# More units of a convolution channel-major, output copies on two engines, taps and jobs at other steps, before a SwiGLU block

One core of one Trainium2 chip. The metric is the time of one execution on the device in microseconds (us). Executions in the fast state are compared throughout (the record marks one as slow when it takes over 1.5% more than the fastest of the same kernel; that happened once, in e4_best); every number of a stall or a block is read from the trace of one profiled execution.

## The reference

A causal convolution of 7 taps over x (8 x 4096 x 192), the taps being a softmax over each head's weights (8 heads of 24 channels), then a SwiGLU feed-forward block with a width of 1536:

```python
w = softmax(weight)                        # 8 heads x 7 taps
out = np.einsum('hk,bskhg->bshg', w, x_unf)      # x_unf: 7 shifted copies of zero-padded x
x = out.reshape(32768, 192)
g = x @ w_gate                             # 192 x 1536
silu = g * (1.0 / (1.0 + np.exp(-g)))
return (silu * (x @ w_val)) @ w_out        # 1536 x 192
```

## The kernel before

The 32768 tokens are 64 blocks of 512; four blocks are a unit. A block is worked off in 12 steps ("chunks" of the 1536 columns, step n = 12 b + j): six gate/val matmuls on TensorE, a silu on ScalarE, a product h on VectorE. Behind chunks 1, 4, 7 and 10 stand the acc matmuls ("slots"), which multiply earlier h by w_out.

The convolution runs ahead of the blocks, in two forms. Some units are convolved on TensorE with band matrices. The others, `POOLED`, are channel-major: GpSimd casts x to fp16 in DRAM (`cast_x`), SyncE loads it transposed (`turn_x`), and six jobs per unit compute the taps with a per-channel scale: taps 0 and 3 on ScalarE, 1 and 2 on VectorE, 4 to 6 and all remaining adds on GpSimd. Four copies on SyncE's queue then put a block's result where the matmuls read it (`place`).

Names in the code and the traces: xs is the fp16 x in DRAM, x its transposed tiles, total, part and piece the sums of a job, y the result of a job for a pair of blocks; pxc is what gate and val matmuls read for a channel-major block, xc the same for a unit convolved on TensorE, which passes through DRAM (scr) and is fetched by transposes; sig is the silu, o_sb the output; the picks are small masks for the taps' scales, made once in the start-up.

```python
POOLED = (2, 3, 5, 6, 8, 9, 11, 12, 14, 15)
...
def turn_x(u, i, at):
    ...
    t = cpool.tile([P, TB + XP], fp16, tag=tag, name=tag, bufs=6)
    seq(nc.sync.dma_start_transpose(out=t, in_=rows[:, at : at + P]))
    ...
def planned(v):                      # v: a channel-major unit; s0: its first step
    s0 = ustep * v
    cast, jobs = {2: (19, 44), 3: (40, 60)}.get(v, (s0 - 118, s0 - 95))
    turns = ((0, 0), (0, Q), (2, Q), None, (1, 0), (1, Q), (3, Q), None, (2, 0), (3, 0))
    lead = {2: (33, 1), 3: (49, 1)}.get(v, (cast + 7, 2))    # first step, distance
    # cast at step `cast`, turn m at lead[0] + lead[1] * m, jobs queued at step `jobs`
...
def pooled_work(n, j, busy):         # after each step
    ...
    if not busy:
        ready = dve_steps[0][0] if dve_steps else None
        ahead = act_steps[0][0] if act_steps else n_jobs[0]
        if ready is not None and (j in (4, 10) or (j in (1, 7) and ready < ahead)):
            dve_steps.pop(0)[1]()                            # one tap on VectorE
        if j in (1, 7, 10) and act_steps and (ready is None or ahead < ready + 3):
            act_steps.pop(0)[1]()                            # one tap on ScalarE
...
# slot 4, behind chunk 4: the end of the previous block
seq(nc.scalar.copy(o_sb[:, 0:2, :], acc[b][0]))
seq(nc.scalar.copy(o_sb[:, 2:4, :], acc[b][1]))
```

In these traces the queues go in program order, and one that stands at a wait holds up what is behind it.

Of the kernel before, what the change touches and what calls it, by code (L numbers as in the profile page):

```python
# [10 lines left out]
def kernel(  # L11
# [9 lines left out]
    nc = tc.nc  # L21
    fp32 = mybir.dt.float32
    fp16 = mybir.dt.float16
    i32 = mybir.dt.int32
    AF = mybir.ActivationFunctionType
    ALU = mybir.AluOpType
# [5 lines left out]
    H, K = weight.shape  # L32
    NT = B * S
    Dff = moe_w_gate.shape[1]
    P = 128
    Q = 64
    SL = D // Q
    grp = D // H
    SUBS = 4
    TB = P * SUBS  # L40
# [9 lines left out]
    ER = ((0, 3), (3, 5))  # L50
    XW = 2 * EG * EO
    NU = NT // UT
    POOLED = (2, 3, 5, 6, 8, 9, 11, 12, 14, 15)
    upb = S // UT
    n_blocks = NT // TB
    n_steps = n_blocks * NCH
# [16 lines left out]
    def seq(i):  # L73

        e = i.ins.engine
        if e in last_on:
            tc.add_manual_dep(i.ins, last_on[e].name, NOSYNC, reason="order")
        last_on[e] = i.ins
        return i

    wpool = ctx.enter_context(tc.tile_pool(name="wts", bufs=1))
    cpool = ctx.enter_context(tc.tile_pool(name="conv", bufs=2))
# [29 lines left out]
    def xe_tile(e):  # L112
        xe[e] = cpool.tile([P, 6, D], fp16, tag="xe", name="xe", bufs=4)
# [62 lines left out]
    def load_wo(m):  # L176
        seq(
            nc.gpsimd.dma_start(
                out=wo16[:, E * m : E * m + E, :].rearrange("p e d -> p (e d)"),
                in_=moe_w_out[WF * m : WF * m + WF, :].rearrange(  # L180
                    "(p e) d -> p (e d)", p=P
                ),
            )
        )

    def small(name, shape, dt=fp32):
        return wpool.tile(shape, dt, tag=name, name=name)
# [14 lines left out]
    load_w(2)  # L202
    for m in range(3):
        load_wo(m)
    xe_tile(2)
    xe_load(2)
    xe_tile(3)
# [32 lines left out]
    def make_shift(n):  # L240
# [26 lines left out]
            op=ALU.mult,  # L267
# [8 lines left out]
            op0=ALU.mult,  # L276
# [257 lines left out]
    pick = {}  # L534

    def make_picks():
        for name, first, rows in (("c01", 0, P), ("c2", P, Q)):
            which = small(f"which_{name}", [H, P], i32)
            seq(
                nc.gpsimd.iota(  # L540
                    which,
                    pattern=[[0, P // rows], [1, rows]],
                    base=first,
                    channel_multiplier=-grp,
                )
            )
            low = small(f"low_{name}", [H, P])
            seq(nc.vector.tensor_single_scalar(low, which, 0, op=ALU.is_ge))
            pick[name] = small(f"pick_{name}", [H, P], fp16)
            seq(  # L550
                nc.vector.scalar_tensor_tensor(
                    pick[name], which, float(grp), low, op0=ALU.is_lt, op1=ALU.mult
                )
            )

# [40 lines left out]
    def turn_x(u, i, at):  # L596
        rows = xs[u][TB * i : TB * i + TB + XP]
        tiles = (x01, x12)[at // Q]
        tag = f"x{at // Q}"
        t = cpool.tile([P, TB + XP], fp16, tag=tag, name=tag, bufs=6)  # L600
        seq(nc.sync.dma_start_transpose(out=t, in_=rows[:, at : at + P]))
        tiles[u, i] = t

# [111 lines left out]

    def planned(v):
        s0 = ustep * v
        cast, jobs = {2: (19, 44), 3: (40, 60)}.get(v, (s0 - 118, s0 - 95))
        turns = (
            (0, 0), (0, Q), (2, Q), None, (1, 0), (1, Q), (3, Q), None, (2, 0), (3, 0)  # L720
        )
        lead = {2: (33, 1), 3: (49, 1)}.get(v, (cast + 7, 2))
        plan.setdefault(cast, []).append(lambda: cast_x(v))
        for m, turn in enumerate(turns):
            if turn:
                todo = lambda turn=turn: turn_x(v, *turn)
            else:
                todo = lambda i=m // 4: join_x(v, i)
            plan.setdefault(lead[0] + lead[1] * m, []).append(todo)
        plan.setdefault(jobs, []).append(lambda: queue_jobs(v))  # L730

    def pooled_work(n, j, busy):
        step_now[0] = n
        if not busy:
            ready = dve_steps[0][0] if dve_steps else None
            ahead = act_steps[0][0] if act_steps else n_jobs[0]
            if ready is not None and (
                j in (4, 10) or (j in (1, 7) and ready < ahead)
            ):
                dve_steps.pop(0)[1]()  # L740
            if j in (1, 7, 10) and act_steps and (ready is None or ahead < ready + 3):
                act_steps.pop(0)[1]()
        while placing:
            u, i = placing[0]
            need = (u, "block", i), (u, "pair", i % 2)
            if not all(job in finished for job in need):
                break
            done = max(finished[job] for job in need)
            if n < max(done + 14, ustep * u + NCH * i - 16):
                break  # L750
            placing.pop(0)
            place(u, i)
# [72 lines left out]
    def slot(k, b, after=None, between=None):  # L825

        if k == 1:
            acc[b] = [
                apool.tile([P, 2, D], fp32, tag=f"acc{i}", name=f"acc{i}")
                for i in range(2)  # L830
            ]
            down(b, [(False, G[0])], 1, after)
            if between is not None:
                between()
            down(b, [(False, G[1])], 1, None)
        elif k == 2:
            down(b, [(True, G[0]), (True, G[1])], 0, after)
            if between is not None:
                between()
            if b < n_blocks - 1:  # L840
                down(b, [(False, G[2])], 0, None)
        elif k == 3:
            down(b, [(True, G[2])], 1, after)
            if between is not None:
                between()
            down(b, [(False, G[3])], 1, None)
        else:
            down(b, [(True, G[3])], 0, after)
            o_sb = hpool.tile([P, SUBS, D], fp32, tag="o_sb", name="o_sb", bufs=3)
            seq(nc.scalar.copy(o_sb[:, 0:2, :], acc[b][0]))  # L850
            seq(nc.scalar.copy(o_sb[:, 2:4, :], acc[b][1]))  # L851
            t0 = b * TB
            seq(
                nc.sync.dma_start(
                    out=out[t0 : t0 + TB, :].rearrange("(s p) d -> p s d", p=P),
                    in_=o_sb,
                )
            )
            del acc[b]
# [26 lines left out]
    for n in range(n_steps):  # L886
        b, j = divmod(n, NCH)
        u, ls = divmod(n, ustep)
        work = None
        if n in (12, 19):  # L890

            def work(e=2 if n == 12 else 3):
                early(e, (gate_bank, gate_bank, val_bank))

        at = (25, 31) if u == 0 else (10, 22)
        if u + 1 < NU and not pooled(u + 1) and ls in at:

            def work(u=u, hh=at.index(ls)):
                conv_half(u + 1, hh)

        gate_val(n)
        if n == 6:
            early(1, (*acc_banks, gate_bank))
        elif n == 8:
            eturn(1, (*acc_banks, gate_bank))
        elif n in (9, 12, 15, 17):
            k = {9: 1, 12: 2, 15: 3, 17: 4}[n]
            slot(k, 0, silu[n - 1 if k == 4 else n - 2], work)
        elif j % 3 == 1 and n > 18:
            k = {1: 3, 4: 4, 7: 1, 10: 2}[j]  # L910
            slot(k, b - 1 if j < 7 else b, silu[n - 2], work)
        if n == 18:
            eturn(2, (*acc_banks, gate_bank))
        elif n == 20:
            eout(3)
        elif n == 21:
            efetch(3)
        if n == 24:
            make_picks()
        if n == 33:  # L920
            make_channel_taps()
        for job in plan.pop(n, ()):
            job()
        pooled_work(n, j, work is not None)
        if u + 1 < NU and not pooled(u + 1):
            if ls == at[0]:
                conv_dup(u + 1)
            if ls == at[1]:
                for m in range(2):
                    conv_out(u + 1, m)  # L930
            if ls == at[1] + 1:
                for m in range(2, 8):
                    conv_out(u + 1, m)
            lo = 32 if u == 0 else 28
            if ls in range(lo, lo + 12, 3):
                fetch(UB * (u + 1) + (ls - lo) // 3)
        if u + 2 < NU and not pooled(u + 2):
            if ls == (21 if u == 0 else 1):
                x16_tile(u + 2)
                load_x(u + 2, 0, silu[n - 1])  # L940
            if ls == (23 if u == 0 else 5):
                load_x(u + 2, 1, silu[n - 1])
            if ls == (37 if u == 0 else 26):
                dup_x(u + 2)
# [42 lines left out]
```

## Time and profile before

| | before |
|---|---|
| time, median of 3 (range) | 792.96 us (792.71 to 793.93) |
| span of the profiled execution | 791.8 us |
| 64 blocks of 11.73 us | 750.7 us |
| stalls behind chunk 7 | 11.7 us, in 24 blocks |

From the page of the kernel before: busy time of each engine, the granted clock in 40 slices (9 is 90% or more), and four groups of instructions (count, then busy time and mean ns of one, then idle time of the engine ahead of them):

```profile
span 791.8 us, 27799 instructions
...
PE 775.6 (98%) x11371; PEld 521.7 (66%) x11371; DVE 638.4 (81%) x949; ACT 588.6 (74%) x1054; POOL 500.7 (63%) x485
...
PEclk9999999999999999999999999999999999999999
...
L792 PE MATMUL acc<-wo,h 64*128 64x192 f16 x6096 | 300.4, 243 | 9.8 <-DVE h L777 7.9
...
L651 DVE SCALAR_TENSOR_TENSOR total<-x,both_taps,total 128x512 f32<-128x512 f16 x120 | 130.4, 1087 | 0.0
...
L676 ACT ACTIVATE total<-x,both_taps 128x512 f32<-128x512 f16 x60 | 42.8, 714 | 2.6 <-DMA x<-xs 2.6
...
L851 ACT COPY o_sb<-acc 128x384 f32<-128x384 f32 x63 | 30.6, 486 | 0.0
```

TensorE is busy for 98% at full clock; no other engine is near its limit on average. What can be had is in the stalls and in TensorE's own share of the convolution. 120 taps stand on VectorE at a mean of 1.09 us, and ScalarE waits once for a transposed x (2.6 us).

### The profile page before, as it was taken

The page shows a single profiled execution, that of the slowest core. Times are in us where ns is not written, and L with a number is a line of the kernel's source. Part 1 is how long each engine was busy: PE and PEld are TensorE (multiplying, and loading weights), DVE is VectorE, ACT ScalarE, POOL GpSimd, SP SyncE. Part 2 cuts the span into 40 slices and gives each one's busy share as a digit, 9 for nine tenths or more (in the row PEclk, how much of TensorE's full clock was granted, in tenths as well). Part 3 has the DMA queues.
Part 4 walks back from the last instruction along what each step waited for, and adds up shares of the span by engine and source line. Part 5 has one row for each costly group of instructions (what it writes and reads, how often), then busy time and mean ns, then how long its engine had stood idle before and what let it go on. Part 6 is the DMA issues. An engine that isn't in the chain of part 4 may idle for free.

```text
span 791.8 us, 27799 instructions
## 1 busy us (share of the span) xinstructions
PE 775.6 (98%) x11371; PEld 521.7 (66%) x11371; DVE 638.4 (81%) x949; ACT 588.6 (74%) x1054; POOL 500.7 (63%) x485
## 2 busy tenths in 40 slices
PE   8999999999999999999999999999999999999997
PEld 5666666666666666666666666666666666666665
DVE  6677889888888867888896688898767888886665
ACT  6677787877878767777876678788668787876664
POOL 8102999996899920589995047899802689990000
PEclk9999999999999999999999999999999999999999
DMA  9965538355642394386129638631862653221211
GB/s 140 177 141 99 124 106 166 83 123 129 115 109 69 56 201 109 94 130 133 39 68 174 117 83 155 107 92 46 146 144 78 150 123 76 68 64 40 68 55 41
DMA packets 159840, 83.90 MB, mean 106 GB/s; under 512 B 102552, under 2 KB 159136, under 8 KB 159136
## 3 DMA queue, kind: packets, MB, share of 16 engines
q1 hardware_dynamic: 139216, 65.58, 35.4%
q0 software_dynamic: 20496, 16.54, 15.0%
q8 instruction: 89, 1.46, 0.8%
q14 instruction: 39, 0.32, 0.1%
HBM read 33.08 MB, written 38.60 MB: 91 GB/s over the span
## 4 chain that ended last, share of the span: by engine, by line
PE 94%; DVE 2%; issue 1%; SPq 1%; DMA 0%; ACT 0%; DVEq 0%; ACTq 0%
PE gate L766 60%; PE acc L792 30%; DVE h L777 2%; PE val L766 2%; PE cv L462 1%; PE warm L867 1%; DMA x<-xs 0%; SPq L520 0%; PE turn L431 0%; PE cv L373 0%; SPq L498 0%; PE acc L813 0%; ACT tme L391 0%; ACT wide L331 0%; ACT sig L775 0%
## 5 line engine op out<-in xcount | busy, mean ns | idle before, releaser
L777 DVE TENSOR_TENSOR h<-sig,val 128x512 f16<-128x512 f16 x768 | 500.0, 685 | 143.5 <-PE val L766 123.1
L775 ACT ACTIVATE sig<-gate 128x512 f16<-128x512 f32 x768 | 455.3, 599 | 183.0 <-PE val L766 155.9
L766 PEld LDWEIGHTS <-w 64*128 64x128 f16 x4608 | 255.6, 110 | 182.3 <-issue 1.5
L766 PE MATMUL val<-pxc,w 64*128 64x512 f16 x1440 | 337.2, 376 | 0.0
L766 PE MATMUL gate<-pxc,w 64*128 64x512 f16 x1440 | 337.2, 376 | 0.0
L792 PE MATMUL acc<-wo,h 64*128 64x192 f16 x6096 | 300.4, 243 | 9.8 <-DVE h L777 7.9
L792 PEld LDWEIGHTS <-h 64*128 64x128 f16 x6096 | 257.7, 94 | 73.9 <-DVE h L777 13.3
L766 PE MATMUL val<-xc,w 64*128 64x512 f16 x864 | 203.6, 376 | 0.3 <-DVE h L777 0.3
L766 PE MATMUL gate<-xc,w 64*128 64x512 f16 x864 | 203.6, 376 | 0.0
L626 POOL TENSOR_TENSOR total<-total,piece 128x512 f32<-128x512 f32 x120 | 158.4, 1320 | 10.0
L641 POOL TENSOR_SCALAR piece<-x,both_taps 128x512 f32<-128x512 f16 x180 | 146.1, 812 | 0.0
L651 DVE SCALAR_TENSOR_TENSOR total<-x,both_taps,total 128x512 f32<-128x512 f16 x120 | 130.4, 1087 | 0.0
L626 POOL TENSOR_TENSOR total<-total,part 128x512 f32<-128x512 f32 x60 | 81.0, 1349 | 69.6 <-DVE total L651 53.9
L490 POOL COPY tm<-tm 128x1280 f16<-128x1280 f16 x5 | 6.2, 1249 | 125.5 <-DVE tm L479 125.5
L626 POOL TENSOR_TENSOR pxc<-total,piece 128x512 f16<-128x512 f32 x40 | 55.8, 1396 | 3.3
L676 ACT ACTIVATE total<-x,both_taps 128x512 f32<-128x512 f16 x60 | 42.8, 714 | 2.6 <-DMA x<-xs 2.6
L676 ACT ACTIVATE part<-x,both_taps 128x512 f32<-128x512 f16 x60 | 42.8, 714 | 0.0
L851 ACT COPY o_sb<-acc 128x384 f32<-128x384 f32 x63 | 30.6, 486 | 0.0
L850 ACT COPY o_sb<-acc 128x384 f32<-128x384 f32 x63 | 30.2, 479 | 0.1
L626 POOL TENSOR_TENSOR y<-total,piece 128x512 f16<-128x512 f32 x20 | 25.7, 1287 | 1.7
L479 ACT CAST tm<-cv 128x480 f16<-128x480 f32 x20 | 10.2, 562 | 6.8 <-PE cv L462 6.8
L479 DVE CAST tm<-cv 128x480 f16<-128x480 f32 x20 | 12.2, 651 | 0.5
(68 smaller groups left out, 88.4 us busy)
## 6 DMA issues: line engine op xcount, KB each, us to landing
out_dram<-o_sb SPq DMA_DIRECT2D x63, 384.0 KB
pxc<-pxc SPq DMA_DIRECT2D x80, 64.0 KB
pxc<-y SPq DMA_DIRECT2D x80, 64.0 KB
x<-in_x_dram POOLq DMA_DIRECT2D x10, 480.0 KB, 9.7
scr<-tm SPq DMA_DIRECT2D x35, 130.0 KB
xs<-in_x_dram POOLq DMA_DIRECT2D x5, 774.0 KB, 7.0
xs<-in_x_dram POOLq DMA_DIRECT2D x5, 768.0 KB, 10.4
x<-x SPq DMA_DIRECT2D x8, 480.0 KB
```

Source lines behind the costliest of these rows:

```text
L462: nc.tensor.matmul(banks[r][32 * c : 32 * c + 32, t * w : t * w + w], band[Q * r : Q * r + Q, h, :], x16[u][Q * r : Q * r + Q, NG * c : NG ...
L479: eng(tm[u][:, NG * r : NG * r + NG, 2 * grp * hp : 2 * grp * hp + 2 * grp].rearrange("p g (t e) -> p g t e", t=2), banks[r][:, 0 : 2 * w] ...
L626: nc.gpsimd.tensor_tensor(job["dst"] if k == K - 1 else total, total, part, op=ALU.add)
L641: nc.gpsimd.tensor_scalar(part, shifted(k), scalar1=job["tap"][:, k : k + 1], scalar2=1.0, op0=ALU.mult, op1=ALU.mult,)
L651: nc.vector.scalar_tensor_tensor(job["total"], shifted(k), job["tap"][:, k : k + 1], job["total"], op0=ALU.mult, op1=ALU.add,)
L676: nc.scalar.activation(part, shifted(k), AF.Copy, scale=job["tap"][:, k : k + 1])
L766: nc.tensor.matmul(o, w16[m][p0 : p0 + Q, k, e::E], xc[b][k][p0 : p0 + Q, 0:TB], start=(k == 0), stop=(k == SL - 1),)
L775: silu[n] = seq(nc.scalar.activation(sg, g, AF.Silu)).ins
L777: seq(nc.vector.tensor_tensor(hj, sg, v, op=ALU.mult))
L792: nc.tensor.matmul(acc[b][bank][:, s, :], hj[p0 : p0 + Q, ts(2 * bank + s, P)], wo16[p0 : p0 + Q, j, :], start=(not second and j == 0 and ...
L850: seq(nc.scalar.copy(o_sb[:, 0:2, :], acc[b][0]))
L851: seq(nc.scalar.copy(o_sb[:, 2:4, :], acc[b][1]))
```

## The change

Its intent: let VectorE compute h without a tap in the slot where TensorE waits for it; to make up for this, move one of the two output copies to VectorE and let taps stand behind chunks 1, 7 and 10 alone; convolve one unit more off TensorE; issue casts and jobs later relative to their use, so that a larger buffer of transposed x (8 in place of 6) is filled no earlier than needed. The core of the diff (the cut parts move the pick masks' first operation to GpSimd and the picks to later steps):

```diff
-    POOLED = (2, 3, 5, 6, 8, 9, 11, 12, 14, 15)
+    POOLED = (2, 3, 4, 6, 7, 8, 10, 11, 12, 14, 15)
...
-        t = cpool.tile([P, TB + XP], fp16, tag=tag, name=tag, bufs=6)
+        t = cpool.tile([P, TB + XP], fp16, tag=tag, name=tag, bufs=8)
...
-        cast, jobs = {2: (19, 44), 3: (40, 60)}.get(v, (s0 - 118, s0 - 95))
+        cast, jobs = {2: (21, 54), 3: (50, 72)}.get(v, (s0 - 112, s0 - 89))
...
-        lead = {2: (33, 1), 3: (49, 1)}.get(v, (cast + 7, 2))
+        lead = {2: (42, 1), 3: (60, 2)}.get(v, (cast + 7, 2))
...
-            if ready is not None and (
-                j in (4, 10) or (j in (1, 7) and ready < ahead)
-            ):
+            if j in (1, 7, 10) and ready is not None:
...
-            seq(nc.scalar.copy(o_sb[:, 2:4, :], acc[b][1]))
+            seq(nc.vector.tensor_copy(o_sb[:, 2:4, :], acc[b][1]))
```

More of the change, by code (lines that the diff above doesn't have):

```diff
@@ L204 @@
         load_wo(m)
+    which = {}
+    above = {}
+    for name, first, rows in (("c01", 0, P), ("c2", P, Q)):
+        which[name] = small(f"which_{name}", [H, P], i32)
+        seq(
+            nc.gpsimd.iota(
+                which[name],
+                pattern=[[0, P // rows], [1, rows]],
+                base=first,
+                channel_multiplier=-grp,
+            )
+        )
+        above[name] = small(f"above_{name}", [H, P])
+        seq(nc.gpsimd.tensor_single_scalar(above[name], which[name], 0, op=ALU.is_ge))
     xe_tile(2)
@@ L536, in make_picks @@
     def make_picks():
-        for name, first, rows in (("c01", 0, P), ("c2", P, Q)):
-            which = small(f"which_{name}", [H, P], i32)
-            seq(
-                nc.gpsimd.iota(
-                    which,
-                    pattern=[[0, P // rows], [1, rows]],
-                    base=first,
-                    channel_multiplier=-grp,
-                )
-            )
-            low = small(f"low_{name}", [H, P])
-            seq(nc.vector.tensor_single_scalar(low, which, 0, op=ALU.is_ge))
+        for name in which:
             pick[name] = small(f"pick_{name}", [H, P], fp16)
@@ L551, in make_picks @@
                 nc.vector.scalar_tensor_tensor(
-                    pick[name], which, float(grp), low, op0=ALU.is_lt, op1=ALU.mult
+                    pick[name], which[name], float(grp), above[name],
+                    op0=ALU.is_lt, op1=ALU.mult,
                 )
@@ L917 @@
             efetch(3)
-        if n == 24:
+        if n == 34:
             make_picks()
-        if n == 33:
+        if n == 37:
             make_channel_taps()
```

## The prediction

> **What bounds the kernel now.** I read the chain that ended last first: nearly all of it is TensorE.
>
> ```profile
> PE 94%; DVE 2%; issue 1%; SPq 1%; DMA 0%; ACT 0%; DVEq 0%; ACTq 0%
> ```
>
> So only what makes TensorE wait, or what it no longer has to do, counts. In the timeline of TensorE I took the starts of the gate/val matmuls. The program has 64 blocks of 12 steps; a step is six 64-row matmuls (0.645 us), and behind chunks 1, 4, 7 and 10 of a block stand 24, 12, 24 and 36 acc matmuls (0.99, 0.50, 0.99, 1.49 us). A block without any stall takes 11.73 us, and from block 5 on every block longer than that has one of two reasons.
>
> First, 24 blocks stall in the slot behind chunk 7, on the h of chunk 5. VectorE, then TensorE, in block 13:
>
> ```profile
> 176.30 1.99 DVE L777 TENSOR_TENSOR h<-sig,val 128x512 f16<-128x512 f16 x3 [0.29 <-PE val L766]
> 178.20 1.73 DVE L651 SCALAR_TENSOR_TENSOR total<-x,both_taps,total 128x512 f32<-128x512 f16 x1
> 179.86 1.87 DVE L777 TENSOR_TENSOR h<-sig,val 128x512 f16<-128x512 f16 x3
> ```
> ```profile
> 179.21 0.99 PE L792 MATMUL acc<-wo,h 64*128 64x192 f16 x20
> 180.59 0.34 PE L792 MATMUL acc<-wo,h 64*128 64x192 f16 x4 [0.40 <-DVE h L777]
> ```
>
> The tap of 1.73 us sits between h4 and h5, where the acc slot is shortest; h5 comes late and TensorE waits. An undisturbed tap takes 0.745 us. Comparing taps and stalls of all blocks, the stall is the tap's time less 1.18 us; their sum is 11.7 us. Second, a unit convolved on TensorE lengthens two blocks by 0.63 us each.
>
> The start-up has one more stall, of 1.28 us at 64.8 us: ScalarE, in order, stands at the first job's first tap until the first transposed x has landed, and the silu behind it waits too.
>
> ```profile
> 64.81 0.72 ACT L676 ACTIVATE total<-x,both_taps 128x512 f32<-128x512 f16 x1 [2.64 <-DMA x<-xs]
> ```
>
> That transpose is late because of the SyncE queue, which works off one 1.26 us transpose after another:
>
> ```profile
> 47.77 8.82 SPq L498 DMA_DIRECT2D scr<-tm  x8
> 56.63 0.37 SPq L506 DMA_DIRECT2D scr<-tm  x1
> 57.05 3.74 SPq L520 DMA_TRANSPOSE xc<-scr  x3
> 60.88 4.54 SPq L601 DMA_TRANSPOSE x<-xs  x3
> 65.47 3.87 SPq L520 DMA_TRANSPOSE xc<-scr  x3
> ```
>
> Last, what costs nothing now but is close. GpSimd's queue, then SyncE's, around the cast of unit 5:
>
> ```profile
> 148.19 1.59 POOL L626 TENSOR_TENSOR pxc<-total,piece 128x512 f16<-128x512 f32 x1
> 149.72 0.57 POOL L586 DMA_DIRECT2D xs<-in_x_dram  x1
> ```
> ```profile
> 144.66 0.59 SPq L700 DMA_DIRECT2D pxc<-pxc  x1
> 156.34 3.78 SPq L601 DMA_TRANSPOSE x<-xs  x3
> 161.69 0.47 SPq L605 DMA_DIRECT2D x<-x  x1
> 162.26 0.96 SPq L854 DMA_DIRECT2D out_dram<-o_sb  x1
> 163.32 3.85 SPq L601 DMA_TRANSPOSE x<-xs  x3
> 167.28 0.52 SPq L700 DMA_DIRECT2D pxc<-pxc  x1
> ```
>
> The cast is emitted at step 122 (about 138.6 us) but goes out only after the jobs ahead of it on GpSimd, 11.1 us later; it lands at 156.3. SyncE stood 11 us at unit 5's first transpose, and behind six of these came the four placing copies of block 13, done at 169.7 and landed about 171.2. The block starts at 172.5: some 1 us to spare.
>
> **What the Trainium skill says.** "SBUF — State Buffer", section "SBUF: two separate sides": VectorE and GpSimd hold a shared port pair as an exclusive lock for a whole instruction; a VectorE operation with two SBUF inputs needs it. The trace agrees: taps (two SBUF inputs) take 739 to 1827 ns and, when slow, as long as the rest of GpSimd's running add (1.27 us) plus 0.55; h, with one input in PSUM, stays at 668 to 690. The copy out of acc reads PSUM, so it should not be disturbed (0.557 us at L952). "DMA: Bandwidth & Descriptors", section "DMA Transpose (X-bar)": plain transposes go from SyncE or ScalarE only; all 143 here stand in SyncE's queue. "Anatomy of one DMA — SWDGE (gpsimd) path" there: waits happen on the issuing sequencer before dispatch; the 11 us above show it. "TensorE: Matmul & The Clock Gate", Part 1: an idle window of about 3.4 us can halve the clock until TensorE has been busy as long; no stall in this trace is that long.
>
> **The change, part by part.**
>
> 1. *No tap behind chunk 4.* The 11.7 us go. The 132 taps (12 a unit, 11 units) stand behind chunks 1, 7, 10 as 47, 44, 41. Chunks 7 and 10 have slack: h8 is wanted only after the 1.49 us slot. Behind chunk 1 the free stretch is 0.99 + 0.645 - 0.60 (one h back to back), so h2 is late by the tap less 1.11 us (seen: 204 ns at a tap of 1314). val has three buffers, so chunk 5 needs h2 gone: h2 ends 1.726 us after chunk 2's last matmul started, chunk 5 starts at 2.003, and a released matmul starts 0.06 after. So a tap behind chunk 1 stalls TensorE by its time less 1.33. GpSimd is busy nearly all the time; a job is four adds of 1.27 and three products of 0.69, 7.4 us alone. At a random moment the rest of the operation exceeds 0.78 with chance 4 x 0.49 / 7.4 = 0.26, by 0.25 on average: 0.065 us x 47 = 3 us back.
>
> 2. *Output copies.* 63 copies of 0.49 leave ScalarE; VectorE gets 63 x 0.557 = 35 us. Behind chunk 4 it has 0.50 + 1.93 for three h of 0.60 and the copy, 2.36. The next use of the bank is 2.65 us after chunk 4's last matmul, the copy ends near 2.3. No gain or loss of its own, and h5 starts 0.1 earlier.
>
> 3. *One PE unit fewer* (1, 5, 9, 13 instead of 1, 4, 7, 10, 13): -1.26.
>
> 4. *Picks on GpSimd.* Two VectorE operations of 0.21 go, two of 0.28 move from step 24 to 34. The 0.44 us stall at step 26 goes.
>
> 5. *First jobs later.* The old stall (-1.28) goes. But unit 2's transposes now stand behind all four fetches of unit 1: SyncE reaches the fetches at 56.6, 12 x 1.30 plus an output issue (0.5) and some 0.4 of waits takes it to 73; issue 1.3, landing 2.3 and release 0.4 give 77. The first tap moves only from step 46 to 55, which ScalarE reaches at 70.5. It waits 6.5 us. TensorE has 0.9 of slack, less than in the kernel before, where 2.64 of wait cost 1.28: stall 5.4.
>
> 6. *Casts closer to their use.* Three units in a row leave GpSimd no rest, and the cast now has 28 steps to the second block of the unit two before it, not 34.
>  - Unit 4: cast at step 80, behind job 2 (last tap at 79). Counted from step 79: job ready 3.0, done 10.9, landing 6.6 to 10.7 later (the nine casts after the first here, mean 8.3), so 19.2. Six transposes 7.8, join with its wait 2.0, output 0.5, placing 2.5 and 1.6: 33.6. Block 9 starts 29.1 after step 79. Stall 4.3.
>  - Unit 6: cast at step 176 behind job 14, GpSimd then about 3 us behind (8.05 us a job against 7.8 between jobs); all else the same distance: stall about 6.5.
>  - Units 8 and 12: only three transposes precede the placing of blocks 25 and 41: 0 to 2 each, 0.5 together.
>  - Units 7, 10, 11, 14, 15: no placing behind them, or an idle GpSimd.
>
> 7. Three stalls now exceed or near the 3.4 us window: about 2 us for a halved clock (estimate from that page: 3.4/2 at most each).
>
> Sum: -11.7 - 1.26 - 0.44 - 1.28 + 3 + 5.4 + 4.3 + 6.5 + 0.5 + 2 = +7.0; 793 + 7 = 800. I take 799. The queue steps of 5 and 6 are hand-stepped with durations of this trace; the same stepping puts the placing of the kernel before within 1 us of the trace (167.3 against 168.0).
>
> **Rivals.** (a) The queues keep up: 5 and 6 are wrong, only 3 us of part 1 come back, 793 - 14.7 + 3 = 781. For it: the settings look tuned (eight x buffers instead of six). Against it: the spare 1 us above. (b) VectorE becomes the bound: 12 x 0.60 + 3 x 1.1 + 0.52 = 11.0 of 11.73 us a block, on average not; with every tap at 1.75 it would be 13, and 44 blocks at +1 make about 815 with part 6. The moment of a tap in GpSimd's cycle wanders by 0.8 us every two blocks, so I hold it unlikely. (c) Part 6 doubles: a cast landing at 10.7 and five units late instead of two, about 808.
>
> **Range and chances.** Even (a) at its best, no stall but the start-up's rest, gives 778; 777.1 would be 2% faster, so that is nearly out. 808.8 is 2% slower and needs (b) or (c). 80%: 785 to 808, the low end standing for half of parts 5 and 6 missing.
>
> **What would show it.** Blocks of 11.73 us with no wait on h behind chunk 7; waits of val matmuls on h at chunk 5; DVE o_sb copies near 0.56 us; ScalarE waiting 6 us on the transposed x near 70 us; TensorE waiting on the placing copies at the starts of blocks 9 and 17 (near 131 and 212 us), with SyncE standing 10 us or more at the transposes before; slices of PEclk below 9. If none of these last three is there, rival (a) holds and my reading of the queues is wrong.

## The result, and the profile after

After takes 805.11 us (median of 4, 801.22 to 806.21); before took 793.44 us (median of 4, 792.71 to 793.97) beside it. The ratio is 1.0139, 95% interval 1.0104 to 1.0174: slower by 1.4%, within 2%. Ratios here are the mean time of one kernel's runs over that of the other's of the same rounds, so not quite the ratio of the quoted medians.

The page of the kernel after, the same parts, and the gate matmuls, which now show idle time ahead of them:

```profile
span 803.2 us, 27838 instructions
...
PE 780.6 (97%) x11307; PEld 602.9 (75%) x11307; DVE 678.0 (84%) x1018; ACT 585.2 (73%) x999; POOL 548.4 (68%) x523
...
PEclk9998999999979999999999999999999999999999
...
L768 PE MATMUL gate<-pxc,w 64*128 64x512 f16 x1584 | 375.7, 378 | 8.4 <-DMA pxc<-pxc 8.0
...
L794 PE MATMUL acc<-wo,h 64*128 64x192 f16 x6096 | 335.6, 244 | 7.1 <-ACT sig L777 5.8
...
L655 DVE SCALAR_TENSOR_TENSOR total<-x,both_taps,total 128x512 f32<-128x512 f16 x132 | 143.3, 1086 | 0.0
...
L680 ACT ACTIVATE total<-x,both_taps 128x512 f32<-128x512 f16 x66 | 47.1, 714 | 6.8 <-DMA x<-xs 6.8
...
L853 DVE COPY o_sb<-acc 128x384 f32<-128x384 f32 x63 | 34.6, 549 | 0.0
```

The waits have changed their releaser. Before, acc waited for h, from VectorE; now it waits for one silu (5.8 us), and gate waits for the placing copies (8.0 us). The clock has two slices below 9. The taps are as long as before (1086 against 1087 ns). The copies take 549 ns on VectorE.

Where the time went is plainest in the starts of the blocks (first gate matmul, us from the span's start), read from TensorE's timelines. The last column is from a later experiment, e4_best_again, and is used there.

| start of block | before | after | after - before | e4_best_again |
|---|---|---|---|---|
| 4 | 63.52 | 63.09 | -0.4 | 62.14 |
| 5 | 76.52 | 82.72 | +6.2 | 73.87 |
| 10 | 136.54 | 146.89 | +10.3 | 132.52 |
| 18 | 234.05 | 252.44 | +18.4 | 228.07 |
| 32 | 402.17 | 417.63 | +15.5 | 393.47 |
| 63 | 774.06 | 785.75 | +11.7 | 760.53 |

After loses 18.4 us in its first 18 blocks and regains 6.7 in the other 45. The loss lies almost wholly in blocks 4, 9 and 17, which take 19.63, 17.00 and 22.60 us in place of 11.73 (block 17 has 0.63 of convolution on TensorE in it). From block 5 on, no block stalls behind chunk 7 any more.

Block 4, in after. SyncE's queue, then ScalarE, then TensorE (start and duration in us, then in brackets the wait ahead and its releaser):

```profile
56.35 12.71 SPq L534 DMA_TRANSPOSE xc<-scr  x9
...
69.79 4.93 SPq L534 DMA_TRANSPOSE xc<-scr  x3
74.81 3.82 SPq L605 DMA_TRANSPOSE x<-xs  x3
```
```profile
77.38 0.72 ACT L680 ACTIVATE total<-x,both_taps 128x512 f32<-128x512 f16 x1 [6.84 <-DMA x<-xs]
```
```profile
78.64 3.06 PE L794 MATMUL acc<-wo,h 64*128 64x192 f16 x36 [5.79 <-ACT sig L777]
```

Twelve transposes of unit 1 stand ahead of unit 2's first one, which goes out at 74.8. ScalarE, in order, waits 6.84 us for it; the silu behind waits too, and TensorE waits for that silu. The 36 acc matmuls then take 3.06 us in place of 1.49 to 1.66: the clock has halved.

Block 9, in after. GpSimd, SyncE, TensorE:

```profile
110.69 1.27 POOL L630 TENSOR_TENSOR pxc<-total,piece 128x512 f16<-128x512 f32 x1
111.90 0.56 POOL L590 DMA_DIRECT2D xs<-in_x_dram  x1
```
```profile
111.57 0.60 SPq L704 DMA_DIRECT2D pxc<-pxc  x1
119.15 1.15 SPq L605 DMA_TRANSPOSE x<-xs  x1
...
120.98 2.67 SPq L605 DMA_TRANSPOSE x<-xs  x2
...
126.59 3.82 SPq L605 DMA_TRANSPOSE x<-xs  x3
130.51 0.54 SPq L704 DMA_DIRECT2D pxc<-pxc  x1
```
```profile
132.52 0.37 PE L768 MATMUL gate<-pxc,w 64*128 64x512 f16 x1 [2.07 <-DMA pxc<-pxc]
```

The cast of unit 4, emitted at step 80 (about 102 us), goes out at 111.90, behind a job. SyncE stands from 112.2 to 119.15 at the first transpose of that cast. Behind six transposes comes the placing of block 9 at 130.51, when the block has already begun (129.89). Block 17 has the same picture with the cast of unit 6 and a wait of 5.92 us.

The granted clock around block 4 and around block 17, in after (columns: stretch, its length, busy time and count of PE, PEld, DVE, ACT, POOL, granted clock, DMA share, GB/s):

```profile
core 0: us, PE busy (x) PEld busy (x) DVE busy (x) ACT busy (x) POOL busy (x), PEclk, DMA share, GB/s
62.00:86.00 24.00, 18.21 (x236) 12.26 (x232) 11.87 (x19) 11.09 (x20) 0.00 (x0) 0.86 0.53 101
222.00:250.00 28.00, 21.89 (x278) 14.66 (x275) 16.59 (x26) 14.67 (x26) 17.76 (x17) 0.82 0.52 115
```

### The profile page after: what moved, and what is told of

Read it like the earlier page. It is cut to its first block, busy times and chain, and to the rows that moved or that the text cites. A ratio compares the mean times of both kernels' runs of the same rounds, so it can differ in the third digit from the quotient of the medians.

```text
span 803.2 us, 27838 instructions
## 1 busy us (share of the span) xinstructions
PE 780.6 (97%) x11307; PEld 602.9 (75%) x11307; DVE 678.0 (84%) x1018; ACT 585.2 (73%) x999; POOL 548.4 (68%) x523
## 4 chain that ended last, share of the span: by engine, by line
PE 92%; POOL 4%; DMA 1%; issue 1%; DVE 1%; SPq 0%; ACT 0%; POOLq 0%; ACTq 0%
PE val L768 40%; PE acc L794 31%; PE gate L768 20%; POOL total L630 2%; POOL piece L645 1%; PE cv L476 1%; DVE h L779 1%; DMA pxc<-y 1%; PE warm L869 0%; PE turn L445 0%; DMA x<-xs 0%; PE cv L387 0%; SPq L704 0%; PE acc L815 0%; DMA pxc<-pxc 0%
## 5 line engine op out<-in xcount | busy, mean ns | idle before, releaser
L768 PEld LDWEIGHTS <-w 64*128 64x128 f16 x4608 | 340.3, 110 | 149.9 <-issue 18.1
L768 PE MATMUL gate<-pxc,w 64*128 64x512 f16 x1584 | 375.7, 378 | 8.4 <-DMA pxc<-pxc 8.0
L768 PE MATMUL val<-pxc,w 64*128 64x512 f16 x1584 | 374.2, 378 | 0.9 <-DMA pxc<-pxc 0.3
L794 PE MATMUL acc<-wo,h 64*128 64x192 f16 x6096 | 335.6, 244 | 7.1 <-ACT sig L777 5.8
L794 PEld LDWEIGHTS <-h 64*128 64x128 f16 x6096 | 305.4, 95 | 37.5 <-ACT sig L777 6.8
L630 POOL TENSOR_TENSOR total<-total,piece 128x512 f32<-128x512 f32 x132 | 179.4, 1359 | 11.0
L768 PE MATMUL gate<-xc,w 64*128 64x512 f16 x720 | 170.6, 377 | 0.0
L768 PE MATMUL val<-xc,w 64*128 64x512 f16 x720 | 170.0, 377 | 0.2
L655 DVE SCALAR_TENSOR_TENSOR total<-x,both_taps,total 128x512 f32<-128x512 f16 x132 | 143.3, 1086 | 0.0
L853 DVE COPY o_sb<-acc 128x384 f32<-128x384 f32 x63 | 34.6, 549 | 0.0
L852 ACT COPY o_sb<-acc 128x384 f32<-128x384 f32 x63 | 30.3, 481 | 0.5
```

The costliest lines, as they stand in the source:

```text
L630: nc.gpsimd.tensor_tensor(job["dst"] if k == K - 1 else total, total, part, op=ALU.add)
L655: nc.vector.scalar_tensor_tensor(job["total"], shifted(k), job["tap"][:, k : k + 1], job["total"], op0=ALU.mult, op1=ALU.add,)
L768: nc.tensor.matmul(o, w16[m][p0 : p0 + Q, k, e::E], xc[b][k][p0 : p0 + Q, 0:TB], start=(k == 0), stop=(k == SL - 1),)
L794: nc.tensor.matmul(acc[b][bank][:, s, :], hj[p0 : p0 + Q, ts(2 * bank + s, P)], wo16[p0 : p0 + Q, j, :], start=(not second and j == 0 and ...
L853: seq(nc.vector.tensor_copy(o_sb[:, 2:4, :], acc[b][1]))
```

## The experiments

The theory after the result: the tap rule gains what was predicted, and the kernel is slower because three inputs come late (the first transposed x of unit 2, the placing of block 9 behind the cast of unit 4, that of block 17 behind the cast of unit 6), each followed by a stretch at half clock. Rivals: the tap rule gains less; the copy on VectorE costs something; the slow stretches are late inputs and no clock.

**e1_turns_early, e2_casts_early, e3_both, b1_tap_rule** ran on one chip; before had a median of 793.38 us there (791.67 to 796.16, 7 runs). e1 puts unit 2's transposes back to their old steps:

```diff
-        lead = {2: (42, 1), 3: (60, 2)}.get(v, (cast + 7, 2))
+        lead = {2: (33, 1), 3: (60, 2)}.get(v, (cast + 7, 2))
```

> Only unit 2's transposes go back to step 33, between the fetches of unit 1; first job stays at step 54. Queue theory: the transpose lands near 65 us, before ScalarE reaches the first tap at 70 us; the 6.8 us wait and block 4's length of 19.6 us go (to about 11.7), blocks 9 and 17 keep their stalls, since they are fixed by job and cast steps; about 805 - 7.9 = 797 us. VectorE theory (three taps and a copy a block are too much for VectorE): the start-up stall goes as well, but it says nothing more. GpSimd theory (eleven units on GpSimd are too many): blocks 9 and 17 as in the changed kernel.

795.89 us (794.32 to 799.33), ratio to before 1.004 (1.0003 to 1.0077). Block 4 takes 11.73 us: the start-up wait was what the transposes' place made it. But block 8, which takes 11.98 in after, takes 14.41. TensorE, then SyncE:

```profile
112.11 0.37 PE L768 MATMUL gate<-pxc,w 64*128 64x512 f16 x1 [1.45 <-DMA pxc<-pxc]
```
```profile
101.99 2.61 SPq L605 DMA_TRANSPOSE x<-xs  x2
104.65 0.54 SPq L583 DMA_DIRECT2D xs<-fill  x1
105.30 0.47 SPq L704 DMA_DIRECT2D pxc<-pxc  x1
105.81 5.46 SPq L704 DMA_DIRECT2D pxc<-y  x2
```

The blocks now start 8 us earlier, but the placing of block 8 starts behind the start-up's transposes and ends at 111.9, after the block's start at 110.1. The two copies out of y held the queue for 5.46 us (the median of the 44 such pairs is 1.23, the next longest 3.17); at the median the placing would have been out before the block began. What held them can be read from the DMA packets: the cast of unit 4 went out at 104.16 and landed at 111.92, and from 105.5 to 109.5 us its queue moved 0.79 MB in packets of 24 KB, which took 2.2 us each, while SyncE's queue got 20 packets of at most 256 bytes through. So here a cast in flight made a small copy late. Part of the start-up wait had hidden that.

e2 sends the casts from unit 4 on six steps earlier and leaves the transposes where they were:

```diff
-        cast, jobs = {...}.get(v, (s0 - 112, s0 - 89))
+        cast, jobs = {...}.get(v, (s0 - 118, s0 - 89))
-        lead = {2: (42, 1), 3: (60, 2)}.get(v, (cast + 7, 2))
+        lead = {2: (42, 1), 3: (60, 2)}.get(v, (s0 - 105, 2))
```

> Only the casts are emitted six steps earlier (118 before the unit instead of 112), the transposes stay at the same steps. Queue theory: the cast then stands ahead of one more 8 us job on GpSimd and lands 8 us earlier; block 9's stall (3.5 us and its clock) goes, block 17's shrinks from 7.4 to 0-2 us, blocks 25 and 42 are 11.73; the start-up stall stays; about 805 - 5.3 - 9 - 0.7 = 790 us. VectorE theory and GpSimd theory: the load of both engines is the same, so blocks 9 and 17 stay long and the time stays within 2 us of 805.

788.88 us (787.68 to 791.32), ratio 0.9956 (0.9921 to 0.9992). Block 17 takes 12.37 us in place of 22.60, block 9 13.02 in place of 17.00, with nothing changed but when the cast goes out. Blocks 9 and 17 were the casts. (Not all of the gain is theirs: block 4 takes 17.53 us here and 19.63 in after, as the start-up wait varies from run to run.)

e3 is both edits (casts at s0 - 118, unit 2's transposes from step 33, other units' at s0 - 105).

> Both edits together. Queue theory: effects add, about 782 us (780 to 785), no slice of the clock below 9, no wait over 2 us on the placing copies. VectorE or GpSimd theory: stays above 793 us, the kernel before.

786.83 us (785.03 to 789.11), ratio 0.9922 (0.9889 to 0.9955), 5 us slower than expected. All of it is block 8, at 16.8 us: its placing goes out behind the start-up's transposes at 110.26, after the block's start at 109.94, with a halved clock behind it. One of these transposes held the queue for 4.37 us instead of 1.26, again with the cast of unit 4 in flight (94.6 to 102.6 us). I had taken the three late inputs for independent; they follow one another on SyncE's queue, and the cast holds that queue up as well.

b1 is the kernel before with the new tap rule alone:

```diff
-            if ready is not None and (
-                j in (4, 10) or (j in (1, 7) and ready < ahead)
-            ):
+            if j in (1, 7, 10) and ready is not None:
```

> The kernel before with only the tap rule of the change (taps behind chunks 1, 7, 10, none behind 4). Theory: the 24 stalls behind chunk 7, 11.7 us, go; stalls of val matmuls at chunk 5 of 1 to 3 us come instead; start-up stall of 1.3 us stays; about 783 us (781 to 786). Rival (VectorE's load is what stalls, wherever the taps stand): the load is unchanged, so the time stays at 793.

785.12 us (784.80 to 785.49), ratio 0.9899 (0.9873 to 0.9924). All 24 stalls behind chunk 7 are gone, 11.7 us; val matmuls wait for h2 at chunk 5 in eight blocks, 2.9 us together (before: none), and block 13 loses 1.3 us at its start, with a wait of 0.94 for a placing copy. From b1's page:

```profile
L790 PE MATMUL acc<-wo,h 64*128 64x192 f16 x6096 | 325.1, 243 | 0.0
```

The tap rule's gain is as the prediction had it, and its price is of the size predicted. The stall at step 26 (0.44 us) stays, so in after it was not the tap rule that removed it; the picks' move, which takes VectorE's work out of these steps, is the likely cause, though no run tests it alone. The start-up stall of 1.28 us is gone in b1 as well, though the first jobs stand where they stood: SyncE's first eight stores took 7.53 us there and 8.82 in the trace of before, and ScalarE waited 0.39 us and not 2.64. That stall varies from run to run.

**b2_copy_alone, w_warm_fill, e4_best, e5_best_copies_on_scalar** ran on another chip (before 793.70, 792.03 to 795.23, 11 runs). b2 is the kernel before with the copy's move alone:

```diff
-            seq(nc.scalar.copy(o_sb[:, 2:4, :], acc[b][1]))
+            seq(nc.vector.tensor_copy(o_sb[:, 2:4, :], acc[b][1]))
```

> Before, with only the second output copy on VectorE. VectorE then has tap and copy (549 ns) behind chunk 4 in the blocks where before puts a tap there (44 of them). My theory: that is why the tap rule goes together with the move; h5 comes later by the copy, the stalls behind chunk 7 grow from 11.7 us by about 0.5 us for each of the 44 blocks less what ScalarE's earlier silu gives back (about 0.1 us each): 805 to 815. Rival: VectorE's queue has the slack, because the copy takes the place of waiting for silu 5: within 3 us of before (791 to 796).

803.06 us (801.70 to 803.86), ratio 1.0117 (1.0103 to 1.0131), a little under the range. Stalls behind chunk 7 grow to 43 and 21.3 us, which is 9.5 more than before; the median is 9.4 more. VectorE and TensorE in block 7 of b2, a block without a stall in before:

```profile
106.56 0.55 DVE L851 COPY o_sb<-acc 128x384 f32<-128x384 f32 x1
107.03 1.47 DVE L651 SCALAR_TENSOR_TENSOR total<-x,both_taps,total 128x512 f32<-128x512 f16 x1
108.42 1.27 DVE L777 TENSOR_TENSOR h<-sig,val 128x512 f16<-128x512 f16 x2
```
```profile
109.15 0.34 PE L792 MATMUL acc<-wo,h 64*128 64x192 f16 x4 [0.60 <-DVE h L777]
```

Copy and tap stand between two h, and h5 comes late by both. The tap rule and the copy's move belong together: with a tap behind chunk 4 the copy costs its own time.

w_warm_fill is after, with zero matmuls in TensorE's three long waits, written into columns of an accumulator bank that nobody reads. It takes no wait away:

```diff
+    def idle_fill(b, count):
+        for _ in range(count):
+            seq(nc.tensor.matmul(spare[b], fill, fill, start=False, stop=False,
+                                 skip_group_check=True))
...
+        if n in (108, 204):
+            idle_fill(b - 1, {108: 32, 204: 86}[n])
         gate_val(n)
...
+            if n == 58:
+                idle_fill(b, 84)
             slot(k, b - 1 if j < 7 else b, silu[n - 2], work)
```

> After, with zero matmuls of 128 columns on TensorE in its three long waits (84 before the matmuls that wait at step 58, 32 before chunk 0 of block 9, 86 before chunk 0 of block 17), into columns of the accumulator bank that nobody reads. They fill 3.5 to 6 us of each wait and take away no wait. My theory, by which the halved clock behind the three waits costs 1.8 to 2.9 us each (6.6 us in all): the same waits end at the same times, the blocks after them run at full speed, 5 to 6.5 us faster than after, 798.5 to 800. Rival: what looks like a halved clock is the queues catching up (inputs that come late one after another): no gain, 804 to 806.

802.21 us (799.46 to 807.16, 6 runs), ratio 1.0111 (1.0084 to 1.0138): 2.9 us under after's median of the other job, half of what I expected; the runs scatter by 7.7 us, and this difference alone would prove little. The trace tells more. Windows of w_warm_fill around blocks 4 and 17, then TensorE and ScalarE in block 4:

```profile
62.00:86.00 24.00, 23.19 (x343) 17.73 (x340) 13.54 (x22) 13.03 (x23) 1.69 (x2) 1.00 0.61 104
222.00:250.00 28.00, 26.20 (x406) 19.65 (x402) 16.53 (x25) 14.16 (x25) 18.57 (x20) 0.94 0.50 112
```
```profile
73.55 4.86 PE L882 MATMUL acc<-fill 128*128 128x128 f16 x84
78.55 1.66 PE L795 MATMUL acc<-wo,h 64*128 64x192 f16 x36
```
```profile
77.28 0.72 ACT L680 ACTIVATE total<-x,both_taps 128x512 f32<-128x512 f16 x1 [6.00 <-DMA x<-xs]
```

In block 4 ScalarE still waits 6.00 us and gets to its tap 14.3 us after the block's start, as in after, but the clock stays at 1.00 (after: 0.86), the 36 acc matmuls take 1.66 us and not 3.06, and the block 17.71 us, 1.92 less than in after. That is no luck of the start-up: from that tap's start to the block's end it is 3.41 us in both runs with a fill, and 5.34 in after and 5.07 in e2 without one. There the rival is out: the slow stretch came from TensorE's idling. The rest of the miss is another late input: as block 4 ends 2 us earlier, block 8 finds a placing copy missing, and blocks 8 and 9 together take 28.68 us, against 28.98 in after. SyncE, then TensorE, at block 8 of w_warm_fill:

```profile
109.39 1.37 SPq L704 DMA_DIRECT2D pxc<-y  x2
110.80 0.59 SPq L704 DMA_DIRECT2D pxc<-pxc  x1
117.88 0.37 PE L768 MATMUL gate<-pxc,w 64*128 64x512 f16 x1 [1.24 <-DMA pxc<-y]
```

All four copies were issued by 111.4, 4.5 us before the block's start, so it was not the order of SyncE's queue. They landed late: the cast of unit 4 was in flight from 109.91 to 117.66, and from 112.0 to 113.5 us no packet of SyncE's queue started. This is e1's hold again. At block 17 the fill ended 1.05 us before the input; with three gaps of 0.25 us behind it the clock fell all the same (0.94).

w2_warm_fill_longer (a third job; before 793.61 us, 792.13 to 794.58, 11 runs, shared with the next two) fills that too: 106 matmuls in place of 86, and six more ahead of each late matmul.

> w_warm_fill with 106 zero matmuls in place of 86 before chunk 0 of block 17 and 6 more before each of that chunk's three late matmuls, because in w_warm_fill the fill ended 1.05 us before the first late input and three gaps of 0.25 us followed, after which the clock fell for 3.5 us all the same. My theory, that gaps in TensorE's work and not the inputs cause the slow stretch: granted clock 1.00 in 222 to 250 us (0.94 in w_warm_fill, 0.82 in after), 1 to 2.5 us faster than w_warm_fill, 799.5 to 801.5. Rival: the slow stretch comes from the late inputs: unchanged, clock 0.94 or less, 802 to 804.

803.72 us (799.58 to 807.50, 6 runs), ratio 1.0118 (1.0088 to 1.0149): no gain, clock 0.94 in 222 to 250 us. A miss. The input came later in this execution, so that 1.07 us of wait were left after the fill, and the clock was halved from 237.8 us on for 3.41 us; at block 8 two waits of 0.83 and 1.16 us, close behind one another, were followed by a half clock as well. So at block 17 the clock's share is not isolated by an experiment; what stands is the doubled distance of the matmuls in the traces.

e4_best takes the late inputs away: casts from unit 4 on 12 steps earlier than after's, unit 2's transposes at e1's steps, and the transposes of units 3 and 4, whose first taps are not needed before steps 103 and 151, behind the placings that they held up.

```diff
-        cast, jobs = {...}.get(v, (s0 - 112, s0 - 89))
+        cast, jobs = {...}.get(v, (s0 - 124, s0 - 89))
-        lead = {2: (42, 1), 3: (60, 2)}.get(v, (cast + 7, 2))
+        lead = {2: (33, 1), 3: (86, 2), 4: (110, 2)}.get(v, (s0 - 105, 2))
```

> After, with every cast at step s0 - 124 (after: s0 - 112), transposes of units from 6 on at s0 - 105 as in after, unit 2's transposes one step apart from step 33, unit 3's from 86 and unit 4's from 110, i.e. behind the placings of blocks 8 and 9, whose start the runs before this one found delayed by them. My theory (the whole loss is three kinds of late input, the wait for unit 2's first transposes, for the cast before unit 4 and for the cast of unit 10, plus the halved clock behind each; e3_both kept 5 us of it because unit 3's transposes stood before block 8's placing): none of these waits is left, blocks 4, 8, 9 and 17 take 12.7 us at most (17: 11.73 + 0.63), span 775 to 778 and time 777 to 780, ratio to before 0.980. Rival: SyncE's queue is so full in the start-up that the delay only moves again, to block 10 or 12: time 783 to 787, with a stall of over 2 us at a block start after 8.

780.88 us as the median of five, ratio 0.9839 (0.9826 to 0.9851), 1 us above the expected range. Four runs lie between 780.40 and 781.48. The profiled one took 1644.5. From the page of that execution:

```profile
PE 1637.1 (100%) x11307; PEld 811.0 (49%) x11307; DVE 685.3 (42%) x1018; ACT 587.1 (36%) x999; POOL 510.1 (31%) x523
...
L768 PE MATMUL gate<-pxc,w 64*128 64x512 f16 x1584 | 777.2, 678 | 0.0
```

TensorE was busy throughout with matmuls of 678 ns in place of 376; VectorE and ScalarE were as fast as ever. It was TensorE's speed and no wait; what slowed it is not known. The kernel again, unchanged, on another chip:

> The kernel of e4_best once more, unchanged, because its profiled execution ran at half speed throughout (1644.5 us against 780 to 781 in the four others) and left no usable profile. Time 780 to 782; in the profile, as in e5's, no block start after block 4 with a stall over 0.5 us, block 4 with about 0.7, and chunk-5 waits of 1 to 2 us in all. Rival: the half-speed execution belongs to this kernel (something in it lets TensorE's clock fall at the start): it comes again, 1640.

780.92 us (779.73 to 781.69, 4 runs), ratio 0.9840 (0.9827 to 0.9854), and no execution at half speed among the four. Its page:

```profile
span 778.0 us, 27832 instructions
...
PE 771.0 (99%) x11307; PEld 603.1 (78%) x11307; DVE 676.4 (87%) x1018; ACT 585.1 (75%) x999; POOL 551.1 (71%) x523
...
PEclk9999999999999999999999999999999999999999
...
L768 PE MATMUL gate<-pxc,w 64*128 64x512 f16 x1584 | 371.2, 376 | 0.0
...
L680 ACT ACTIVATE total<-x,both_taps 128x512 f32<-128x512 f16 x66 | 47.1, 713 | 0.0
```

No wait for placings (after: 8.4 us of idle ahead of these gate matmuls), none for the transposed x (6.8), full clock. Blocks 4, 8 and 9 take 11.73 us each, block 17 12.37. The placing of block 8 goes out at 94.0 us, 11 before e1's. What is left is 1.7 us of val waits at chunk 5. This kernel is 1.6% faster than before and, over two jobs, 3% faster than after. It differs from after only in the steps of casts and transposes: these cost after 24 us. Earlier casts and another order of the transposes came together here, and no run tells which of them ended block 8's wait; the cast of unit 4 is in flight from 85.2 to 92.8 us, clear of that placing.

e5 is e4_best with both output copies on ScalarE:

```diff
-            seq(nc.vector.tensor_copy(o_sb[:, 2:4, :], acc[b][1]))
+            seq(nc.scalar.copy(o_sb[:, 2:4, :], acc[b][1]))
```

> The kernel of e4_best with both output copies back on ScalarE. My theory, by which the copy's move is worth almost nothing in time, as neither engine sets the end once no tap stands behind chunk 4: within 1.5 us of e4_best, with ScalarE 35 us busier and VectorE 35 us less. Rival: the second copy on ScalarE (0.55 us behind the first) delays silu 5 or 6 and the taps of chunk 4's neighbours, so that TensorE waits about 0.2 us per block, 8 to 12 us slower than e4_best.

780.32 us (779.80 to 780.92), ratio 0.9833 (0.9821 to 0.9846), 0.6 us from e4_best. Once no tap stands behind chunk 4, it doesn't matter where the copy is.

e6 is e5 with the units of before:

```diff
-    POOLED = (2, 3, 4, 6, 7, 8, 10, 11, 12, 14, 15)
+    POOLED = (2, 3, 5, 6, 8, 9, 11, 12, 14, 15)
```

> The kernel of e5_best_copies_on_scalar with the unit set of before (2, 3, 5, 6, 8, 9, 11, 12, 14, 15: ten channel-major units, six on TensorE in place of five). My theory: one more unit's convolution on TensorE costs 1.26 us (two halves of 0.63), less one unit's share of the chunk-5 waits (0.1 us): 1 to 1.5 us slower than e5 in the same rounds, 781.4 to 782. Rival: the unit set is what makes casts and placings late (unit 10 right behind 8 with unit 9's loads between), so that the old set gains: 0 to 2 us faster than e5.

782.25 us (781.53 to 782.96), ratio 0.9858 (0.9845 to 0.9872): 1.3 us slower than e4_best_again of the same job. e5 ran in the other job; against its 780.32 it is 1.9. By the steps of the two traces, the halves convolved on TensorE take 1.35 us more. The term of 1.26 us for one unit less on TensorE has the right size.

## Why the prediction was right or wrong

799 us was predicted with a range of 785 to 808; 805.11 came. That it would stay within 2%, and the places of the loss, were right; the sum is 6 us too small. Term by term, from the traces of before and after:

| term | predicted | measured in after | how known |
|---|---|---|---|
| no tap behind chunk 4 | -11.7 | -11.7 | no stall behind chunk 7; b1 |
| waits of val at chunk 5 | +3 | +1.7 | nine blocks; 2.9 in eight in b1 |
| one unit fewer on TensorE | -1.26 | -0.5 | eight halves of 0.64 before; six in after, four of them 0.81 to 0.84. e6 gives 1.3 to 1.9 for the unit |
| picks | -0.44 | -0.44 | stall at step 26 gone; stays in b1 |
| old start-up stall | -1.28 | -1.28 | but varies by run (b1) |
| start-up wait, block 4 | +5.4 | +5.95 | e1 removes it |
| block 9 | +4.3 | +3.5 | e2 removes most of it |
| block 17 | +6.5 | +7.4 | e2 removes it |
| blocks 25, 41 and others | +0.5 | +1.2 | 0.47 and 0.19 in blocks 25 and 42; 0.5 more at step 22, which varies by run |
| halved clock | +2 | +6.6 | 1.95, 1.8, 2.8 behind blocks 4, 9, 17 |
| sum | +7.0 | +12.4 | spans: +11.4; another 0.5 was saved before block 4, and the small stalls sum up to 0.4 more or less by what is taken as an undisturbed step |

**The step that failed** is part 7, "about 2 us for a halved clock (estimate from that page: 3.4/2 at most each)". The cost came behind all three stalls and is 6.6 us in place of 2. I had priced it as one event and a little, and held a wait near 3.4 us for a borderline case; the trace shows about 2 us or more behind each, also behind block 9's, whose longest single wait was 2.07 us. "At most" was wrong too: the number is the blocks' excess less their waits, 22.60 - 11.73 - 0.63 - 7.4 = 2.8 for block 17. The clock records of the trace fit: the granted clock is 0.50 for 6.83, 3.41 and 10.24 us around the three waits, and TensorE works in 4.0, 3.4 and 6.9 us of that, of which half is 2.0, 1.7 and 3.5 (an estimate, taking all work as half as fast). For block 4 the fill experiment shows it by itself (5.34 us against 3.41 from the release to the block's end). For 9 and 17 it is read from the traces, and w_warm_fill and w2 could not isolate it.

**Right in mechanism and size:** the gain of part 1, part 2 ("No gain or loss of its own", e4 against e5) and part 5. In part 6 the working held term for term at unit 4: counted from the start of step 79 the cast went out after 11.4 us (10.9 predicted), landed after 18.7 (19.2), the last placed input came after 33.4 (33.6), and the block started after 29.4 (29.1). Two of its differences are off by 0.2: 33.6 - 29.1 is 4.5, not 4.3, and 6.5 of wait less 0.9 of slack is 5.6, not 5.4. Rival (a), that the queues keep up, is what e4_best makes true: 781 was put on it, 780.9 came.

**Right in mechanism, off in size:** the prices of parts 1 and 3. A tap behind chunk 1 stalls TensorE by its time less 1.53 us, not 1.33: in after taps of 1.67 and 1.78 us cost 0.14 and 0.25, in b1 one of 2.52 cost 0.99. What made up for a part of that, the prediction didn't have: four of the halves convolved on TensorE now cost 0.2 us more each (last section). That the two together came near the +3 is partly luck.

**What the prediction didn't see:** the late inputs are not a list of independent sums. With the start-up wait removed, the wait moved to the next placing in SyncE's queue (e1: block 8; e3: 5 us short). And a cast makes inputs late in a second way, by holding up SyncE's copies and transposes while it is in flight. This is read from the traces of e1, e3 and w_warm_fill; no run tests it alone. The larger buffer of transposed x was not tested alone either.

The Trainium skill, "SBUF — State Buffer", section "SBUF: two separate sides", says that the port pair shared by VectorE and GpSimd is held for a whole instruction. The run of b2 agrees: the tap of 1.47 us shown above (0.745 undisturbed) ends 0.55 us after the GpSimd addition that began before it, and the copies out of PSUM keep their 0.55 us, before that tap and everywhere (548 to 558 ns in all 64).

## What to carry to other kernels

Before moving work later on an engine, follow each queue that feeds it in program order: a queue that waits for one late cast holds back copies for blocks that need nothing of it, and a large cast in flight can hold back small copies even when they are issued in time. The cure here was both, earlier casts and another order of the queue. Price a stall of TensorE of two microseconds or more with about another two for the clock, per stall: every stall of 1.79 us or more in these traces had a half clock beside it, and of those of 0.8 to 1.5 us some. And test the parts of a change singly: here the tap rule alone was worth 8 us, and the copy's move alone cost 9.

## What the Trainium skill lacked or had wrong

- "TensorE: Matmul & The Clock Gate", "Part 1: The HAM clock gate": its table gives about 3.4 us idle before the clock halves. Shorter waits were followed by a half clock here: 2.07 us (after, block 9), 1.79 (e3_both, block 8), two of 0.83 and 1.16 close together and one of 1.07 behind a fill (w2_warm_fill_longer); 1.45 us (e1_turns_early, block 8) and 1.26 (start-up of after) were not. The nine stretches at half clock that lie within a run lasted 3.41 us (six), 6.83 (two) or 10.24 (one), which is one, two or three times 3.41. Under "HAM oscillation — how this bites in real kernels", the page's example has 1.67 us at the lower clock for each wait.
- The same page, in its caveats in Part 1, calls the clock records unreliable and names a clock seen stuck for 50 us and more. One execution of e4_best ran at about half speed for its whole 1642.7 us (matmuls 678 ns against 376), and its trace holds no record of a lower clock at all; so the granted clock of 1.0 doesn't rule this state out.
- No page has this: the gate and val matmuls of a pair start 3 to 5 ns apart from block 3 on in before, but in after, e1, e4_best_again and b1 they mostly start alternately, 0.13 to 0.20 and 0.01 to 0.08 us apart. The blocks still take 11.73 us; PEld's busy share rises from 66% to 75% (after) and 78% (e4_best_again). In after it begins at chunk 5 of blocks 6, 18, 34 and 50, in the last three with a wait of val for h2, and ends at the convolved halves in blocks 17, 32 and 48; these, and that of block 16, take 0.81 to 0.84 us and not 0.64. Why is open; it needs no halved clock, as e4_best_again and b1 have none at these places.
- "DMA: Bandwidth & Descriptors", "DMA Transpose (X-bar)": no cost of issue (a table elsewhere on the page, about trn3, has one for earlier chips, in cycles and for small tiles). One transpose of 528 rows by 128 fp16 channels held SyncE's queue for 1.26 us here (three in 3.82); transposes are the largest load of that queue, and the start-up wait is 12 of them.
- The same page, "Anatomy of one DMA — SWDGE (gpsimd) path": its fit, 2.0 us + bytes / 436e3, gives 3.8 us for the 774 KB that a cast writes (an estimate from the page). The median from issue to landing is 7.4 us in after. The casts here go from DRAM to DRAM and change the type; which of this makes the difference is not shown.
- No page has a number for what a large cast in flight does to small copies: a cast of 32 packets of 24 KB, at 2.4 us each, kept SyncE's queue from starting any packet from 112.0 to 113.5 us (w_warm_fill), and a pair of copies that usually holds the queue for 1.23 us held it for 5.46 (e1_turns_early).
